# Gated linear attention ahead of a multiplicative FFN: part 1 in units of two batches and four heads, two positions on a partition, all small products by quarters of the array

## The chip, the cores and the metric

The kernel runs on one core of one Trainium2 chip. The metric is the device time of one execution in microseconds (us). Before the change it is 507.3 us, the median of three runs (506.86 to 508.71). A run counts as slow when it is over 1.5% above the fastest of the same kernel; only fast runs are compared.

Ratios below are the mean time of one kernel's fast runs over the mean of the fast runs of the kernel before from the same rounds, on the same chip, with a 95% interval. They are therefore not quite the ratios of the medians that are quoted beside them.

Names used throughout: TensorE is PE in the profile (PEld its weight loads), VectorE DVE, ScalarE ACT, GpSimd POOL, and SP the engine that here does nothing but issue transfers. A q after the name (SPq, ACTq) is that engine's sequencer. L128 is line 128 of the kernel in question.

## The reference, cut to what matters

```python
# 4 batches, 8 heads, 768 positions, 48 numbers per head
for t in range(S):
    state = alpha[:, :, t, :, None] * state + np.einsum('bhd,bhe->bhde', k[:, :, t], v[:, :, t])
    y[:, :, t] = np.einsum('bhd,bhde->bhe', q[:, :, t], state)
x = y.transpose(0, 2, 1, 3).reshape(3072, 384)
out = ((x @ w1) * (x @ w2)) @ w3 @ w_out          # weights given as float64
```

## The kernel before

Part 1 does the recurrence in chunks of 128 positions. A unit is one batch and one chunk with all eight heads: 24 units. For each unit the logarithms of alpha are summed over the positions with a triangular matrix on TensorE (decays), k and q are scaled by the exponentials, transposed, multiplied (scores), masked, and multiplied with v (attend). The state that comes from earlier chunks adds its part (state) and is brought forward (outer, advance). The results are stored in DRAM (xd) and read back transposed (xT) for the gates, the products x@w1 and x@w2 in three fp32r parts. Gate tiles are slipped between the units to fill TensorE, and the float64 weights (raw) are converted on ScalarE and VectorE meanwhile. What follows part 1 (rest of the gates, the product of w3 and w_out, the projection) keeps its arithmetic; each tile of the output is stored in two transfers where it was one.

```python
def load_kq(n):                                   # one load: 128 positions x 8 heads x 48
    st["kq", n] = inp.tile([C, 2, H, D], FP32, tag="kq", name="kq")
    nc.sync.dma_start(out=st["kq", n][:, 0], in_=rows(k, n))
    nc.sync.dma_start(out=st["kq", n][:, 1], in_=rows(q, n))
...
def decays(n):                                    # one running sum over 128 positions
    lc = bank()[:, 0:DM]
    ...
    if n < LATE:
        nc.tensor.matmul(lc, utri if n % 2 else after, la, start=True, stop=True)
    else:
        for i in range(2):
            nc.tensor.matmul(lc, sums[:, n % 2], la[:, i], start=(i == 0), stop=(i == 1))
...
def attend(n):
    ...
    for i in range(2):
        nc.scalar.copy(x[:, :, i], y[i])
    ...
    for half in range(2):                         # two stores a unit, issued by ScalarE
        nc.scalar.dma_start(out=to[half, :, :, ds(c * C, C)], in_=x[ds(DP * half, D)])
```

A point that matters later: the order in which each engine gets its instructions is laid down when the kernel is built, from an estimate of when each will be ready. It is not simply the order of the program text. TensorE's order here is nearly that of the text (at most one place off); of SP's loads those of the raw weights are put up to 47 places ahead of it, those of q, k, v and alpha at most 8 (all counted on the built program).

Of the kernel before, what the change touches and what calls it, by code (L numbers as in the profile page):

```python
# [46 lines left out]

@with_exitstack
def kernel(
# [19 lines left out]
    NP = H // 2  # L69
# [10 lines left out]
    assert DM <= 512 and TG <= 512  # L80
# [11 lines left out]
    ps = pool("ps", 8, space=PSUM)  # L92
# [6 lines left out]
    work = pool("work", 2, stack=part1, side="right", reuse_waits="tile")  # L99

    def bank():
        return ps.tile([C, 512], FP32, tag="bank", name="bank")
# [6 lines left out]
    ends = {n: dram.tile([3, DM], FP32, name=f"ends{n}") for n in range(2, N, 2) if n % NCH}  # L109
    xd = [dram.tile([DM, TG], FP32, name=f"xd{g}") for g in range(NG)]  # L110
    abd = [dram.tile([C, KF, TG], FP32, name=f"abd{g}") for g in range(NG)]

    vs = [p1.tile([C, H, DP], FP32, name=f"v{i}") for i in range(AHEAD + 1)]
    for x in vs:
        nc.gpsimd.memset(x[:, :, D:], 0.0)

    def rows(src, n):
        b, c = divmod(n, NCH)
        return src[b, :, ds(c * C, C), :].rearrange("h p d -> p h d")

    def load_a(n):
        if n < N:
            st["a", n] = inp.tile([C, H, D], FP32, tag="ac", name="ac")
            nc.sync.dma_start(out=st["a", n], in_=rows(alpha, n))

    def load_kq(n):
        if n >= N:
            return  # L128
        st["kq", n] = inp.tile([C, 2, H, D], FP32, tag="kq", name="kq")
        nc.sync.dma_start(out=st["kq", n][:, 0], in_=rows(k, n))  # L130
        nc.sync.dma_start(out=st["kq", n][:, 1], in_=rows(q, n))

    def load_v(n):
        if n < N:
            st["v", n] = vs[n % len(vs)]
            nc.sync.dma_start(out=st["v", n][:, :, 0:D], in_=rows(v, n))
# [15 lines left out]
    utri = p1.tile([C, C], FP32, name="utri")  # L152
    after = p1.tile([C, C], FP32, name="after")

    sums = p1.tile([C, 2, C], FP32R, name="sums")
    keep = p1.tile([C, C], I32, name="keep")
    qks = [p1.tile([C, 2, H, DP], FP32, name=f"qk{i}") for i in range(3)]
    Ts = [p1.tile([C, NP, DP], FP32, name=f"T{i}") for i in range(2)]
    decs = [p1.tile([C, 3, NP], FP32, name=f"dec{i}") for i in range(2)]

    make_upper_triangular(nc, utri, val=1.0, diag=True)

    nc.vector.tensor_scalar_add(after, utri, -1.0)
    nc.gpsimd.tensor_copy(out=sums[:, 0], in_=after)
    nc.gpsimd.tensor_copy(out=sums[:, 1], in_=utri)
    nc.vector.memset(rebias, -(1023.0 - 127.0) * 2.0 ** 23)

    nc.vector.tensor_scalar_mul(keep, utri, -1.0)
    keep_bc = keep[:, None, :].to_broadcast([C, NP, C])
    for x in qks:  # L170
        nc.vector.memset(x[:, :, :, D:], 0.0)
    make_identity(nc, ident)
    for x in Ts + decs:
        nc.gpsimd.memset(x, 0.0)
# [55 lines left out]
    def last(n):  # L230
        return n % NCH == NCH - 1

    def logs(n):
        if n >= N:
            return
        a = st.pop(("a", n)).rearrange("p h d -> p (h d)")
        la = st["la", n] = work.tile([C, DM], FP32, tag="la", name="la")
        nc.scalar.activation(la, a, AF.Ln)
        if n >= LATE:

            t = st["la", n] = work.tile([C, 2, DM], FP32R, tag="la2", name="la2", bufs=1)
            nc.scalar.copy(t[:, 0], la)
            nc.vector.tensor_sub(t[:, 1], la, t[:, 0].bitcast(FP32))
        if n in ends:
            nc.scalar.dma_start(out=ends[n][2:3], in_=a[0:1])

    def decays(n):
        if n >= N:
            return
        lc = bank()[:, 0:DM]  # L250
        la = st.pop(("la", n))
        if n < LATE:
            nc.tensor.matmul(lc, utri if n % 2 else after, la, start=True, stop=True)
        else:
            for i in range(2):
                nc.tensor.matmul(lc, sums[:, n % 2], la[:, i], start=(i == 0), stop=(i == 1))  # L256

        e = st["e", n] = work.tile([C, 2, DM], FP32, tag="e", name="e", bufs=3)
        nc.scalar.activation(e[:, 0], lc, AF.Exp, scale=-1.0)
        nc.scalar.activation(e[:, 1], lc, AF.Exp)  # L260
        if n in ends:
            nc.scalar.dma_start(out=ends[n][0:1], in_=e[0:1, 0])
        if n + 1 in ends:
            nc.scalar.dma_start(out=ends[n + 1][1:2], in_=e[C - 1:C, 1])

    def decayed(n):
        if n < N:
            nc.vector.tensor_mul(qks[n % 3][:, :, :, 0:D], st.pop(("kq", n)),
                                 st.pop(("e", n)).rearrange("p i (h d) -> p i h d", h=H))

    def load_ends(n):
        if n not in ends:
            return
        with nc.allow_non_contiguous_dma(reason="single values to partitions"):
            for i in range(2):
                nc.scalar.dma_start(out=decs[n // 2 % 2][ds(DP * i, D)].rearrange("d m j -> d (m j)"),
                                    in_=ends[n].rearrange("m (j i d) -> i d (m j)", i=2, d=D)[i])

    def transposed(n):
# [3 lines left out]
        qkT = work.tile([C, 2, NP, C], FP32, tag="qkT", name="qkT")  # L283

        tp = [bank().rearrange("p (i j c) -> p i j c", i=2, j=NP) for _ in range(2)]
        for i in range(2):
            for j in range(NP):
                for half in range(2):
                    s = ds(DP * half, DP)
                    nc.tensor.transpose(tp[half][:, i, j, :], qk[s, i, 2 * j:2 * j + 2, :], ident[s, s])  # L290
        for half in range(2):
            nc.scalar.copy(qkT[:, :, :, ds(DP * half, DP)], tp[half])  # L292
        st["qkT", n] = qkT

    def outer(n):
        if n >= N or last(n):
            return
        qk, vc = qks[n % 3], st["v", n]
        s1 = bank()[:, 0:NP * D].rearrange("p (j d) -> p j d", j=NP)
        for j in range(NP):  # L300
            for i in range(2):
                nc.tensor.matmul(s1[ds(DP * i, DP), j, :], qk[:, 0, 2 * j + i, :], vc[:, 2 * j + i, 0:D],  # L302
                                 start=True, stop=True)

        if n % 2:
            to = st["T", n] = work.tile([C, NP, D], FP32, tag="tmp", name="tmp")
        else:
            to = Ts[1][:, :, 0:D]
        if n % NCH == 0:
            nc.vector.tensor_copy(out=to, in_=s1)  # L310
        else:
            nc.vector.tensor_add(to, s1, Ts[n % 2][:, :, 0:D])

    def advance(n):

        if n not in ends:
            return
        dec, d = work.tile([C, NP], FP32, tag="dec", name="dec"), decs[n // 2 % 2]
        nc.gpsimd.tensor_mul(dec, d[:, 0, :], d[:, 1, :])
        nc.gpsimd.tensor_mul(dec, dec, d[:, 2, :])  # L320
        nc.gpsimd.tensor_tensor(Ts[0][:, :, 0:D], st.pop(("T", n - 1)),
                                dec[:, :, None].to_broadcast([C, NP, D]), op=ALU.mult)

    def scores(n):
        qkT = st["qkT", n]
        sc = [bank().rearrange("p (j c) -> p j c", j=NP) for _ in range(2)]
        for j in range(NP):
            for i in range(2):
                r = ds(DP * i, D)
                nc.tensor.matmul(sc[i][:, j, :], qkT[r, 0, j, :], qkT[r, 1, j, :], start=True, stop=True)  # L330
        ms = work.tile([C, 2, NP, C], FP32, tag="ms", name="ms")
        for i in range(2):
            nc.vector.tensor_tensor(ms[:, i].bitcast(I32), sc[i].bitcast(I32), keep_bc, op=ALU.bitwise_and)  # L333
        st["ms", n] = ms

    HP = NP // 2

    def attend_state(n):
        qkT = st.pop(("qkT", n))
# [3 lines left out]
        y = [bank()[:, 0:HP * C].rearrange("p (j c) -> p j c", c=C) for _ in range(2)]  # L343
        st["y", n] = y, [(half * HP + j, i, y[i][ds(DP * half, DP), j, :])
                         for j in range(HP) for i in range(2) for half in range(2)]
        if n % NCH:
            for j, i, to in st["y", n][1]:
                r = ds(DP * i, D)
                nc.tensor.matmul(to, Ts[n % 2][r, j, :], qkT[r, 1, j, :],  # L349
                                 start=(j % HP == 0), stop=False, skip_group_check=True)  # L350

    def attend(n):
        (y, heads), ms, vc = st.pop(("y", n)), st.pop(("ms", n)), st.pop(("v", n))
        for j, i, to in heads:
            nc.tensor.matmul(to, vc[:, 2 * j + i, :], ms[:, i, j, :], start=(n % NCH == 0 and j % HP == 0),  # L355
                             stop=(j % HP == HP - 1), skip_group_check=True)
        x = work.tile([C, HP, 2, C], FP32, tag="x", name="x")
        for i in range(2):
            nc.scalar.copy(x[:, :, i], y[i])
        x = x.rearrange("p j i t -> p (j i) t")  # L360

        g, c = divmod(n, G)
# [254 lines left out]
```

## Time and profile before

| | before |
|---|---|
| median time | 507.3 us |
| TensorE busy / mean granted clock | 466.6 us / 0.973 |
| VectorE, ScalarE busy | 371.3, 248.1 us |
| TensorE idle in part 1 | 35.6 us, 34.8 of it before 145 us |
| issues of loads of q, k, v, alpha on SP | 96, 84.8 us in all |
| issues by ScalarE in part 1 | 91, 33.2 us in all |
| packets of the inputs | 98,304 of 192 B |

The line below is the stretch from 145 to 212 us, the last 67 us of part 1 (length, then busy us of PE, weight loads, DVE, ACT, POOL, then granted clock, DMA share, GB/s).

```profile
145.00:212.00 67.00, 66.17 (x861) 60.45 (x861) 44.45 (x74) 37.50 (x85) 3.43 (x9) 1.00 0.57 138
```

TensorE is busy 66.17 of 67.00 us at full clock: whatever the transfers do in this stretch costs nothing.

### The profile page before, as it was taken

Reading aid. Unit: us, or ns where it says so; the run is one execution under the profiler, and the core shown is the slowest. Engines: PE = TensorE matmul, PEld = TensorE weight load, DVE = VectorE, ACT = ScalarE, POOL = GpSimd, SP = SyncE. Lnnn points to the kernel's source line nnn. Section 1 sums busy time; section 2 is a strip of 40 time slices with the busy share of each in tenths; the row PEclk is TensorE's granted clock in tenths of the full one; section 3 lists DMA queues with packets and bytes.
Section 4 is the critical chain, followed back from the end, with each engine's and each line's share of the span. In section 5 each row is a group of like instructions: output and inputs, shape, how many; then the busy total and the mean of one; then the engine's idle time right before and its main releaser. Section 6 shows DMA issues by size and latency. Waiting matters only on the chain.

```text
span 506.9 us, 9883 instructions
## 1 busy us (share of the span) xinstructions
PE 466.6 (92%) x3760; PEld 424.8 (84%) x3760; DVE 371.3 (73%) x620; ACT 248.1 (49%) x479; POOL 13.8 (3%) x43
## 2 busy tenths in 40 slices
PE   3777499499799999999999999999999999999997
PEld 1556388398799899899999998898888799999996
DVE  2777789699966767599999976967533497777771
ACT  2665566468557555355555544544323343333330
POOL 2000000010100010000000000000000000000000
PEclk9998599889899999999999999999999999999999
DMA  9999999998879833265565432432001686555511
GB/s 173 182 217 196 256 216 225 194 246 209 166 167 215 194 81 106 79 186 174 177 200 186 160 117 88 142 103 72 33 31 48 171 231 192 174 180 179 174 56 47
DMA packets 168735, 79.10 MB, mean 156 GB/s; under 512 B 112856, under 2 KB 162544, under 8 KB 168688
## 3 DMA queue, kind: packets, MB, share of 16 engines
q1 hardware_dynamic: 147184, 70.73, 54.9%
q10 hardware_dynamic: 21504, 7.75, 6.7%
q8 instruction: 29, 0.48, 0.4%
q14 instruction: 18, 0.15, 0.1%
HBM read 56.40 MB, written 22.06 MB: 155 GB/s over the span
## 4 chain that ended last, share of the span: by engine, by line
PE 71%; DVE 1%; issue 0%; ACT 0%; DVEq 0%
PE bank L387 36%; PE bank L391 18%; PE bank L436 8%; PE bank L355 2%; PE bank L330 2%; PE bank L430 1%; PE bank L349 1%; PE bank L290 1%; PE bank L302 1%; PE bank L256 1%; DVE x L378 1%; DVE x L377 0%; ACT t L389 0%; ACT ab L454 0%; DVE r L392 0%
## 5 line engine op out<-in xcount | busy, mean ns | idle before, releaser
L387 PE MATMUL bank<-x,w 128*128 128x384 f32 x768 | 163.9, 348 | 15.0 <-DVE x L377 8.5
L387 PEld LDWEIGHTS bank<-x,w 128*128 128x128 f32 x768 | 136.5, 192 | 21.1 <-DVE x L377 9.7
L389 ACT ACTIVATE t<-bank 128x384 f32<-128x384 f32 x152 | 73.4, 490 | 119.2 <-PE bank L387 96.7
L392 DVE SCALAR_TENSOR_TENSOR r<-bank,t 128x384 f32<-128x384 f32 x128 | 68.4, 550 | 45.7 <-ACT t L389 37.1
L391 PE MATMUL bank<-x,w 128*128 128x384 f32 x384 | 89.2, 340 | 1.5 <-DVE x L378 1.4
L391 PEld LDWEIGHTS bank<-x,w 128*128 128x128 f32 x384 | 69.2, 191 | 3.1 <-PE bank L387 1.4
L387 PE MATMUL bank<-w3o,ab 128*128 128x384 f32 x384 | 70.6, 335 | 1.0 <-ACT ab L454 1.0
L387 PEld LDWEIGHTS bank<-w3o,ab 128*128 128x128 f32 x384 | 66.8, 188 | 1.4 <-ACT ab L454 1.3
L436 PE MATMUL bank<-wo,w3T 128*128 128x384 f32 x128 | 42.6, 486 | 0.0
L391 PE MATMUL bank<-w3o,ab 128*128 128x384 f32 x192 | 37.1, 334 | 0.0
L436 PEld LDWEIGHTS bank<-wo,w3T 128*128 128x128 f32 x128 | 24.2, 189 | 14.9
L189 ACT ACTIVATE rest<-raw 128x512 f32<-128x512 uint32 (+1 forms) x36 | 23.4, 649 | 26.6 <-DMA raw<-in_moe_w_dram 18.3
L455 DVE TENSOR_TENSOR ab<-abl,ab 128x1024 fp32r<-128x1024 f32 x24 | 29.4, 1223 | 9.1 <-ACT ab L454 9.1
L403 DVE TENSOR_TENSOR ab<-r 128x384 f32<-128x384 f32 x64 | 35.3, 552 | 0.9
L454 ACT ACTIVATE ab<-abl 128x1024 fp32r<-128x1024 f32 x24 | 25.5, 1062 | 20.1 <-PE bank L391 18.8
L330 PEld LDWEIGHTS bank<-qkT 48*128 48x128 f32 x384 | 25.5, 198 | 10.8 <-ACT qkT L292 5.1
L330 PE MATMUL bank<-qkT 48*128 48x128 f32 x384 | 30.7, 298 | 4.2 <-ACT qkT L292 3.7
L333 DVE TENSOR_TENSOR ms<-bank,keep 128x512 int32<-128x512 int32 x48 | 31.2, 682 | 4.2 <-PE bank L330 4.2
L391 PEld LDWEIGHTS bank<-w3o,ab 128*128 128x128 f32 x192 | 33.6, 188 | 0.0
L292 ACT COPY qkT<-bank 128x512 f32<-128x512 f32 x48 | 25.8, 586 | 10.3 <-PE bank L290 8.8
L194 ACT ACTIVATE power<-power,rebias 128x512 uint32<-128x512 uint32 (+1 forms) x36 | 25.0, 696 | 10.3 <-DVE power L193 10.3
L392 DVE SCALAR_TENSOR_TENSOR o<-bank,t 128x384 f32<-128x384 f32 x24 | 13.4, 556 | 22.1 <-issue 13.7
(65 smaller groups left out, 509.7 us busy)
## 6 DMA issues: line engine op xcount, KB each, us to landing
abd<-ab SPq DMA_DIRECT2D x64, 192.0 KB
abl<-abd SPq DMA_DIRECT2D x24, 512.0 KB
raw<-in_moe_w_dram SPq DMA_DIRECT2D x16, 512.0 KB
raw<-in_moe_w_dram SPq DMA_DIRECT2D x24, 256.0 KB
ac<-in_alpha_dram SPq DMA_DIRECT2D x24, 192.0 KB
kq<-in_k_dram SPq DMA_DIRECT2D x24, 192.0 KB
kq<-in_q_dram SPq DMA_DIRECT2D x24, 192.0 KB
v<-in_v_dram SPq DMA_DIRECT2D x24, 192.0 KB
```

The costliest lines, as they stand in the source:

```text
L194: nc.scalar.activation(power, power, AF.Relu, scale=2.0 ** 23, bias=rebias)
L292: nc.scalar.copy(qkT[:, :, :, ds(DP * half, DP)], tp[half])
L330: nc.tensor.matmul(sc[i][:, j, :], qkT[r, 0, j, :], qkT[r, 1, j, :], start=True, stop=True)
L333: nc.vector.tensor_tensor(ms[:, i].bitcast(I32), sc[i].bitcast(I32), keep_bc, op=ALU.bitwise_and)
L387: nc.tensor.matmul(p1, w[part][i], x[part][i], start=(part == i == 0), stop=(part == 1 and i == n - 1))
L389: nc.scalar.activation(t, p1, AF.Copy, scale=(1.0 + 1.0 / P) * scale)
L391: nc.tensor.matmul(p2, w[2][i], x[2][i], start=(i == 0), stop=(i == n - 1))
L392: nc.vector.scalar_tensor_tensor(to, p2, -scale, t, op0=ALU.mult, op1=ALU.add)
L403: nc.vector.tensor_mul(ab, *r)
L436: nc.tensor.matmul(po, w3T[:, j, :], wo[:, j, :], start=(j == 0), stop=(j == KF - 1))
L454: nc.scalar.activation(t[:, 0], ab, AF.Copy, scale=1.0 - 2.0 ** -13)
L455: nc.vector.tensor_sub(t[:, 1], ab, t[:, 0].bitcast(FP32))
```

## The change

Intent: put two neighbouring positions of a batch side by side on a partition, so that a run in DRAM is 384 B and not 192 B; put two batches on the two halves of the partitions, with four heads a unit; then do all small products on quarters of the array, so that TensorE changes its mode less often. y gets two banks of its own, and the schedule of the gates is retuned. The core of the diff:

```diff
-    ps = pool("ps", 8, space=PSUM)
+    ps = [pool("ps", 6, space=PSUM)]
+    yp = pool("yp", 2, stack=part1, space=PSUM)
...
+    def load(dst, src, n):
+        b0, c, hh = n // NU * W, n % NU // 2, n % 2
+        src = src[ds(b0, W), ds(hh * HH, HH), ds(c * C, C), :]
+        for b in range(W):
+            nc.sync.dma_start(out=dst[ds(b * DP, DP)], in_=src[b].rearrange("h (p r) d -> p h (r d)", r=R))
...
-            nc.scalar.dma_start(out=ends[n][2:3], in_=a[0:1])
+            for b in range(W):
+                nc.scalar.dma_start(out=ends[n][2:3, b].rearrange("o (h d) -> o h d", d=D),
+                                    in_=a[b * DP:b * DP + 1, :, 0:D])
...
-            nc.tensor.matmul(lc, utri if n % 2 else after, la, start=True, stop=True)
+        for x in parts:
+            nc.tensor.matmul(lc.rearrange("p (r x) -> p r x", r=R), w[:, 0],
+                             x[:, None, 0:DH].to_broadcast([C, R, DH]), ...)
+        for x in parts:
+            nc.tensor.matmul(lc[:, DH:], w[:, 0], x[:, DH:], ...)
+        for x in parts:
+            nc.tensor.matmul(lc[:, 0:DH], w[:, 1], x[:, DH:], ...)
...
-                nc.tensor.matmul(sc[i][:, j, :], qkT[r, 0, j, :], qkT[r, 1, j, :], start=True, stop=True)
+                        nc.tensor.matmul(sc[i][rows(b), s, j, :], qkT[f, b, 0, j, rows(s)], qkT[f, b, 1, j, :],
+                                         start=True, stop=True)
...
+        for b in range(W):
+            for i in range(2):
+                nc.scalar.dma_start(out=dst[hh, i, b], in_=x[ds(DP * (b ^ i), D), i])
-        for half in range(2):
-            nc.scalar.dma_start(out=to[half, :, :, ds(c * C, C)], in_=x[ds(DP * half, D)])
```

Attend, outer (now called add) and state are cut into quarters in the same way as the scores. The order inside a unit is now: half of the scores, attend of the unit before, the other half, add, state, transposes, gates, decays.

## The prediction

> **What bounds the kernel now.** I read the page's row of slices first, then the busy time by stretches, then who waited for whom, then the timeline of TensorE in one unit of part 1. The slices (12.7 us each):
>
> ```profile
> PE   3777499499799999999999999999999999999997
> DVE  2777789699966767599999976967533497777771
> PEclk9998599889899999999999999999999999999999
> DMA  9999999998879833265565432432001686555511
> ```
>
> Two regimes. In the first ten or eleven slices (to about 130 us) the DMA engines are full, TensorE has holes and its granted clock dips. From there to the end TensorE is at 9 in every slice but the last. Part 1, which the change rewrites, ends at about 212 us, so it lies in both. The other 295 us (the rest of the gates, the fold of w3 and w_out, the projection) are TensorE work that the change leaves alone. The stretches of the first regime:
>
> ```profile
> 20.00:44.00 24.00, 19.62 (x327) 15.34 (x322) 18.86 (x33) 14.45 (x32) 2.06 (x6) 1.00 1.04 196
> 44.00:66.00 22.00, 13.72 (x102) 10.46 (x100) 17.34 (x28) 13.94 (x28) 0.00 (x0) 0.61 1.07 236
> 66.00:88.00 22.00, 21.35 (x277) 19.49 (x268) 19.91 (x38) 15.02 (x34) 0.95 (x3) 1.00 1.10 230
> 88.00:106.00 18.00, 11.00 (x114) 9.16 (x116) 11.98 (x20) 8.12 (x18) 2.53 (x3) 0.81 1.03 199
> 106.00:128.00 22.00, 21.19 (x283) 19.52 (x276) 22.00 (x43) 16.74 (x38) 0.00 (x0) 1.00 0.90 222
> ```
>
> Columns: length, then busy us of PE, weight loads, VectorE, ScalarE, GpSimd, then granted clock, DMA share, GB/s. The holes are in 44 to 66 (8.3 us idle, clock 0.61) and 88 to 106 (7.0 us, 0.81), with DMA over 1.0 in both. What they wait for:
>
> ```profile
> ACT rest L189 <- DMA raw<-in_moe_w_dram: 18.3, 10, 2.8
> ACT la L238 <- DMA ac<-in_alpha_dram: 14.0, 6, 3.1
> DVE mant L190 <- DMA raw<-in_moe_w_dram: 13.0, 4, 4.8
> 57.20 1.33 PE L387 MATMUL bank<-x,w 128*128 128x384 f32 x3 [4.78 <-ACT x L376]
> 100.28 1.33 PE L387 MATMUL bank<-x,w 128*128 128x384 f32 x3 [4.84 <-DVE x L377]
> ```
>
> TensorE waits for the split of x, but the split stands in line on VectorE and ScalarE, whose instructions ahead of it wait for weights or alpha still in transfer. So there DMA is the cause at one remove. TensorE's idle before 145 us, gap by gap, adds up to 34 us; some 10 us more go to a low clock (the 16 score matmuls at 47.59 took 2.08 us, at 66.16 they took 1.16).
>
> The second regime, one unit of part 1:
>
> ```profile
> 190.80 0.51 PE L256 MATMUL bank<-la,sums 128*128 128x384 f32 x2
> 191.23 0.67 PE L349 MATMUL bank<-qkT,T 48*64 48x128 f32 x16
> 191.83 1.16 PE L330 MATMUL bank<-qkT 48*128 48x128 f32 x16
> 192.83 0.66 PE L290 MATMUL bank<-ident,qk 64*128 64x64 f32 x16
> 193.42 1.09 PE L355 MATMUL bank<-ms,v 128*64 128x128 f32 x16
> 194.34 0.62 PE L302 MATMUL bank<-v,qk 128*64 128x48 f32 x16
> 194.90 1.31 PE L387 MATMUL bank<-x,w 128*128 128x384 f32 x6
> ```
>
> Start to start: decays 0.43, state 0.60, scores 1.00, transposes 0.59, attend 0.93, outer 0.55: 4.10 us of small products per unit; the two half gates after them make a unit of 7.3 us, and TensorE has no hole in it.
>
> **What the Trainium skill says.** (1) "DMA: Bandwidth & Descriptors", Specifications: line rate needs transfers of at least 512 B. The trace agrees: the 98,304 packets of 192 B (q, k, v, alpha) took 17.7 ns each, 10.8 bytes per ns; the 33,792 of 512 B took 30.0 ns, 17 bytes per ns. (2) The same page, on why a DMA increments its semaphore by 16: the number of engines is set by the slowest dimension, so a transfer to 64 partitions should still use 16; no run here shows it yet. (3) "TensorEngine Tiling (Array Packing)", Key Properties: changing the tiling mode drains TensorE. The trace agrees: from the last state group (quarters) to the first score (halves) 0.20 us pass, within state a group follows in 0.109. (4) "TensorE: Matmul & The Clock Gate", Part 3: tiles in different places run at once. The trace agrees: in state four quarter matmuls start within 20 ns, the next four 109 ns later; in scores and attend two half-array matmuls per 112 and 109 ns; in outer (48 columns) two per 58 ns.
>
> **The change, part by part.**
>
> *Inputs.* Two positions side by side make runs of 384 B, so 49,152 packets in place of 98,304. On the line through 192 B (17.7 ns) and 512 B (30.0) a 384 B packet is estimated at 25 ns. The inputs then take 49,152 x 25 = 1,230 us of engine time, not 1,743: 32 us less over 16 engines, of which some 20 us before 106 us (about 62,900 of the packets are there). DMA share there falls from about 1.05 to 0.85. Issues on SP double (96 to 192) but each writes a quarter of the descriptors (unloaded issues took 0.37 us, in a full queue 0.7 to 0.8), so SP's time stays.
>
> *Small products by quarters.* An fp32 product is two instructions. Scores go from 16 to 32, attend from 16 to 32, outer from 16 to 32, state stays 16. But each is a quarter of the array, four at a time: scores 8 groups x 0.109 = 0.87 (pure time before 8 x 0.112 = 0.89), attend 0.87 (0.87), state 4 x 0.109 = 0.44, outer 8 groups x 0.058 = 0.46 if four weight loads overlap as well as two do. Total 2.64 against 2.66: **the array gains nothing**. What is gained is a mode: full, quarters, rows, columns, full before (four switches), full, quarters, rows, full after (three). At 0.1 to 0.2 us a switch with its refill that is about 0.2 us a unit.
>
> *Decays.* The running sum over pairs takes three products (384, 192, 192 columns) for one of 384: twice the columns. In fp32 (the first ten units) 2 x 0.32 us become 1.28, +0.64 warm, nearly twice that at a cold clock: +6.4 us, in the first regime, and for units 0 and 1 on the starting chain (L253 took 1.65 us there). In fp32r (14 units) 2 x 0.173 become 0.35 plus four of about 0.09: +0.35 a unit, +4.9 us where TensorE is full.
>
> *State from zeros.* Attend_state now runs for the first units of a batch pair too: 4 x 0.44 = 1.8 us.
>
> Sum in the full regime: a unit goes from 4.10 to about 4.2 us: -0.2 (switch) +0.35 (decays) -0.02; over 14 units about +2, with two of the zero states +3.
>
> *PSUM.* y has two banks of its own; six are left for what used eight with y among them. Attend_state(n) needs both y banks evicted after attend(n-1): half the scores and add lie between, 0.44 + 0.46 = 0.90 us, while the end of the last matmul (0.27) and two copies (0.67) with signals take about 1.05. A wait of 0.1 to 0.3 us a unit, longer where ScalarE is behind: 2 to 4 us.
>
> *ScalarE* issues four stores of x for two and more boundary rows: some 75 issues more at 0.25 to 0.4 us. It was occupied about 70% in part 1 with issues counted, so mostly hidden. VectorE's elements are the same, two small adds for one.
>
> *First regime.* With less DMA the wait for weights at 91 to 95.5 us (4.75) and 52 to 55 us (3.1) should mostly go, and the low clock after them: about 8 to 9 us. The start gains 1 to 2 us in arrivals and loses as much to longer cold decays. The stretch 20 to 44 gains 1 to 2, 66 to 88 and 106 to 128 nothing: TensorE and VectorE (22.00 of 22.00) are full there. Together -11 us after the fp32 decays.
>
> **Sum.** 507 - 11 + 3 + 3 = 502. The schedule was retuned with the change (where gates begin, one extra half gate at two places, four at the end of part 1), which should recover a little of the waits: I say 500.5.
>
> **The rivals.**
> - *DMA was the whole bound of the first regime.* For: share at or above 1.0 to 106 us. Then 20 us come off, and the total is about 490. Against: in that time VectorE had about 76 of 106 us busy and TensorE 75, and both get more to do, so they bind after some 12 us.
> - *VectorE binds first.* For: 22.00 of 22.00 in 106 to 128, and the conversions are paced by units, not by transfers. Then the holes only move, and TensorE's extra work shows: 505 to 508.
> - *TensorE's extra work is larger than I count.* fp32r with 192 columns may not run at the rate of 384 (nothing in the trace has that shape); at a fourth of the rate it adds 14 x 0.9 = 13 us in the full regime: about 514. Or the outer groups fall to two at a time: +0.46 x 20 = 9 us. The order of quarters, pinned in the program, speaks against the second.
> - *PSUM waits.* Six banks in rotation tie the gates to VectorE's masks and ScalarE's copies; 0.5 us a unit would be +12 us. Against: VectorE is 70% busy after 130 us.
>
> **Range and chances.** The mechanism gives 502 with about 7 us either way, mostly from how much of the 44 us of holes and low clock goes. Faster by over 2% means under 497.2; that takes 15 us or more from the first regime, or waits that are nil: 0.33. Slower by over 2% (over 517.4) takes slow fp32r and PSUM waits together: 0.07. Within 2%: 0.60. Eight in ten: 489 to 511.
>
> **What would show it.** Right: 49,152 packets of 384 B near 25 ns; DMA share under 0.9 before 106 us; waits on raw weights and alpha below half of 45 us; a unit after 130 us of 7.3 to 7.6 us with four quarter matmuls per 0.109 us; the three decays at 0.75 to 0.8 us. Wrong: packets of 384 B that take 30 ns or more; fp32r products of 192 columns over 0.2 us apart; holes on TensorE before attend_state or the gates in every unit; the holes at x's split as long as before.

## More of the kernel before

The next line is from the waits of SP's queue (us in total, times, longest).

```profile
SPq L130 <- DMA xd<-x: 5.4, 2, 3.1
```

SP stood 5.4 us in all for the stores of x (xd<-x) that ScalarE issues. That is odd at first sight, since a load needs nothing of a store; keep it in mind. The page's list of transfers gives the size of a load:

```profile
ac<-in_alpha_dram SPq DMA_DIRECT2D x24, 192.0 KB
```

## The result, and the profile after

The changed kernel takes 563.31 us (median of 4 runs, 560.43 to 566.7) where the kernel before takes 507.55 in the same rounds: ratio 1.1099 (1.1032 to 1.1165). It is slower by 11%, and correct.

| | before | after |
|---|---|---|
| span of the profiled run | 506.9 | 562.2 |
| TensorE busy / mean granted clock | 466.6 / 0.973 | 499.4 / 0.946 |
| start of unit 6, 10, 23 (its first scores) | 66.2, 106.3, 205.8 | 76.3, 122.6, 260.0 |
| TensorE idle in part 1 | 35.6 | 58.4 |
| loads of q, k, v, alpha on SP | 96, 84.8 us | 192, 124.9 us |
| issues by ScalarE in part 1 | 91, 33.2 us | 166, 76.8 us |
| packets of the inputs | 98,304 at 17.7 ns | 49,152 at 24.6 ns |

From the start of unit 23 on both kernels need the same time (301 and 302 us), so all of the loss lies in part 1: 16 us of it stand at the start of unit 10, and 38 more come from unit 10 to 23, where 7.7 us a unit became 10.6. The span grew by 55.3 us, of which 32.8 are TensorE busy and 22.5 idle. Of the busy part, up to 17 us is a lower clock: (1 - 0.946) x 562.2 = 30.4 us lost against (1 - 0.973) x 506.9 = 13.7 (an estimate, since some of it falls on idle time).

The slices of the kernel after (14.1 us each), to set beside those of the prediction:

```profile
PE   4767669889788788779999999999999999999996
...
PEclk9797878979898989968999999999999999999999
DMA  5556656555575656631365555433210287566531
```

The DMA engines are no longer full anywhere in part 1: 5 to 7 where there was 9. But TensorE now has holes in the first eighteen slices. Part 1 from 145 us on, in numbers:

```profile
145.00:212.00 67.00, 57.02 (x952) 51.55 (x953) 43.35 (x78) 32.16 (x70) 2.78 (x6) 0.92 0.62 158
212.00:262.00 50.00, 40.30 (x647) 36.07 (x645) 24.26 (x47) 21.49 (x48) 2.02 (x6) 0.86 0.48 132
```

TensorE is busy 57 of 67 us where it was busy 66, at a clock of 0.92 and 0.86 where it was 1.00, and the DMA share is 0.48 to 0.62. None of them is full. One unit, on TensorE (start, length, engine, line, operation; in brackets the idle time ahead of it and what ended it):

```profile
190.03 0.51 PE L278 MATMUL bank<-la,sums 128*128 128x384 f32 x2
...
190.89 0.67 PE L357 MATMUL bank<-qkT 48*64 48x128 f32 x16
191.38 1.05 PE L413 MATMUL y<-ms,v 64*48 64x128 f32 x32
192.25 0.62 PE L357 MATMUL bank<-qkT 48*64 48x128 f32 x16
192.69 0.63 PE L373 MATMUL bank<-v,qk 64*64 64x48 f32 x32
197.62 0.94 PE L402 MATMUL y<-qkT,T 48*64 48x128 f32 x16 [4.30 <-ACT x L418]
```

The products themselves are as predicted: two halves of the scores at 0.49 and 0.44 us, attend 0.87, add 0.45 when nothing stands in its way, the three decays 0.86 start to start. Then comes a hole of 4.3 us ahead of state (L402). The waits of the other engines, over the whole run:

```profile
PE y L402 <- ACT x L418: 22.1, 12, 4.3
...
PE bank L278 <- ACT la L255: 20.8, 7, 5.0
...
ACT rest L209 <- DMA raw<-in_moe_w_dram: 17.5, 13, 2.6
...
ACT la L255 <- DMA ac<-in_alpha_dram: 9.9, 5, 3.3
...
DVE mant L210 <- DMA raw<-in_moe_w_dram: 7.1, 6, 2.6
```

The second line of these is new; the first is what the prediction called the wait for the y banks. But the last three say what stands behind them: ScalarE and VectorE, in line, still wait for loads. Follow the hole at 193 to 197 us back. First ScalarE:

```profile
194.82 0.67 ACT L209 ACTIVATE rest<-raw 128x512 f32<-128x512 uint32 x1 [2.50 <-DMA raw<-in_moe_w_dram]
...
196.50 0.72 ACT L214 ACTIVATE power<-power,rebias 128x512 uint32<-128x512 uint32 x1 [1.00 <-DVE power L213]
197.13 0.62 ACT L418 COPY x<-y 128x256 f32<-128x256 f32 x2
197.51 1.83 ACTq L424 DMA_DIRECT2D xd<-x  x4
```

It copies y (L418) at 197.13, because the two instructions ahead of it, of the conversion of weights, came late: L209 waited 2.50 us for raw weights, L214 another 1.00 for VectorE. The last line is four issues by which ScalarE is held up again, 1.83 us. SP issued these raw weights here:

```profile
187.54 2.09 SPq L128 DMA_DIRECT2D kq<-in_q_dram  x2
189.68 1.08 SPq L201 DMA_DIRECT2D raw<-in_moe_w_dram  x2
```

In the trace the first of the two q loads starts at 187.54, and the store of x that ScalarE had issued at 185.24 landed at 187.52; the second starts at 189.03, and the store issued at 185.66 landed at 189.02. Both times the load and the store raise the same semaphore. So the raw weights were issued at 189.68 and 190.32, the second landed at 194.74, and TensorE stood. The two waits add 0.42 and 0.63 us here, and 4.4 us go from the second issue of the weights to its landing: a single hole doesn't show which of the links counts. What SP waits for, over the whole run:

```profile
SPq L128 <- DMA xd<-x: 20.8, 15, 4.5
...
SPq L128 <- DMA xT<-xd: 8.8, 2, 4.4
SPq L128 <- DMA dec<-ends: 8.1, 4, 3.3
...
SPq L128 <- DMA ends<-e: 6.4, 7, 2.4
```

The issue records name a semaphore for each transfer. SP and ScalarE together use eight, in turn, in the order that the build laid down, and most issues wait for the transfer that used the same one before them (after, 364 of SP's 390 issues and 130 of ScalarE's 170 carry that wait, counted on the built program). In the kernel before, 45 of the 235 issues of part 1 come within 0.5 us of the landing that frees their semaphore; after, 110 of 403 do. The size of a load, and the count:

```profile
ac<-in_alpha_dram SPq DMA_DIRECT2D x48, 96.0 KB
```

Half the bytes each, but the issue is not shorter. A load alone, after a pause on SP, took 0.37 us before and 0.60 after; the mean of all issues is 0.88 and 0.65 us. Four times 0.88 are 3.5 us a unit, eight times 0.65 are 5.2. That alone does not fill SP: it issues for 56% of part 1 both before (118 of 212 us) and after (147 of 262 us). The rest of its time it waits.

### The profile page after: what moved, and what is told of

It reads as the page before. It is cut to its first block, busy times and chain, and to the rows that moved or that the text cites. A ratio compares the mean times of both kernels' runs of the same rounds, so it can differ in the third digit from the quotient of the medians.

```text
span 562.2 us, 12721 instructions
## 1 busy us (share of the span) xinstructions
PE 499.4 (89%) x5008; PEld 454.4 (81%) x5008; DVE 376.5 (67%) x642; ACT 252.6 (45%) x479; POOL 15.4 (3%) x53
## 4 chain that ended last, share of the span: by engine, by line
PE 55%; DVE 0%; issue 0%; DVEq 0%
PE bank L451 30%; PE bank L455 15%; PE bank L500 7%; PE bank L494 1%; PE y L413 1%; PE bank L357 1%; PE y L402 0%; PE bank L341 0%; DVE o L456 0%; DVEq L456 0%
## 5 line engine op out<-in xcount | busy, mean ns | idle before, releaser
L451 PE MATMUL bank<-x,w 128*128 128x384 f32 x768 | 166.7, 352 | 6.9 <-ACT x L440 3.7
L451 PEld LDWEIGHTS bank<-x,w 128*128 128x128 f32 x768 | 138.2, 194 | 13.3 <-ACT x L440 4.7
L456 DVE SCALAR_TENSOR_TENSOR r<-bank,t 128x384 f32<-128x384 f32 x128 | 69.6, 554 | 62.3 <-ACT t L453 37.1
L455 PE MATMUL bank<-x,w 128*128 128x384 f32 x384 | 90.3, 343 | 1.9 <-DVE x L442 1.7
L455 PEld LDWEIGHTS bank<-x,w 128*128 128x128 f32 x384 | 70.5, 194 | 3.5 <-PE bank L451 3.1
L278 PE MATMUL bank<-la,sums 128*128 128x384 f32 x48 | 21.0, 520 | 21.8 <-ACT la L255 20.8
L209 ACT ACTIVATE rest<-raw 128x512 f32<-128x512 uint32 (+1 forms) x36 | 23.4, 650 | 33.6 <-DMA raw<-in_moe_w_dram 17.5
L357 PE MATMUL bank<-qkT 48*64 48x128 f32 x768 | 35.9, 300 | 1.8 <-ACT qkT L344 0.9
L402 PE MATMUL y<-qkT,T 48*64 48x128 f32 x320 | 18.2, 307 | 18.8 <-ACT x L418 18.6
L214 ACT ACTIVATE power<-power,rebias 128x512 uint32<-128x512 uint32 (+1 forms) x36 | 25.0, 697 | 17.4 <-DVE power L213 16.8
```

What stands on the lines that cost most here:

```text
L214: nc.scalar.activation(power, power, AF.Relu, scale=2.0 ** 23, bias=rebias)
L357: nc.tensor.matmul(sc[i][rows(b), s, j, :], qkT[f, b, 0, j, rows(s)], qkT[f, b, 1, j, :], start=True, stop=True)
L451: nc.tensor.matmul(p1, w[part][i], x[part][i], start=(part == i == 0), stop=(part == 1 and i == n - 1))
L455: nc.tensor.matmul(p2, w[2][i], x[2][i], start=(i == 0), stop=(i == n - 1))
L456: nc.vector.scalar_tensor_tensor(to, p2, -scale, t, op0=ALU.mult, op1=ALU.add)
```

## The experiments

Eighteen kernels were run, each with a profile and three rounds. The expectations use letters for the theories: S, the transfers (their number, SP's and ScalarE's issues and the eight shared semaphores); P, TensorE and its hand-overs with ScalarE and VectorE; in the first round also the y banks and the running sums; O and H are told where they come up. The runs are called by their first letter below, the pinned ones (p_) by their order. Results first:

| run | what | us (median) | ratio to before (95%) |
|---|---|---|---|
| (the change) | | 563.31 | 1.1099 (1.1032, 1.1165) |
| a_state_later | state moved behind a half gate | 562.54 | 1.1045 (1.0984, 1.1105) |
| b_one_decay | one running sum of three, wrong | 550.88 | 1.0855 (1.0811, 1.0899) |
| c_stores_pool | stores of x issued by GpSimd | 562.30 | 1.1026 (1.0948, 1.1105) |
| d_raw_pool | raw weights issued by GpSimd | 562.32 | 1.1064 (1.1022, 1.1105) |
| k_one_load | one load for two, wrong | 545.45 | 1.0732 (1.0699, 1.0765) |
| g_act_issues_pool | all ScalarE's issues to GpSimd | 543.61 | 1.0711 (1.0656, 1.0766) |
| m_one_load_pool | k and g together, wrong | 530.59 | 1.0444 (1.0402, 1.0486) |
| u_all_three | k, g and b together, wrong | 532.21 | 1.0477 (1.0428, 1.0526) |
| q_busy | g with idle copies on ScalarE | 566.71 | 1.1146 (1.1101, 1.1192) |
| e_before_split | before, loads in two by partitions | 554.14 | 1.0901 (1.0862, 1.0941) |
| n_split_heads | before, loads in two by heads | 518.27 | 1.0177 (1.0138, 1.0216) |
| o_split_pool | e, second halves by GpSimd | 524.84 | 1.0314 (1.0284, 1.0345) |
| s_before_act_pool | before, ScalarE's issues to GpSimd | 506.13 | 0.9949 (0.9918, 0.9980) |
| p_after_in_k_order | the change in k's order | 579.32 | 1.1356 (1.1288, 1.1423) |
| p_k_in_after_order | k in the change's order | 550.72 | 1.0817 (1.0751, 1.0882) |
| p_e_in_n_order | e in n's order | 544.81 | 1.0718 (1.0661, 1.0774) |
| p_n_in_e_order | n in e's order | 554.57 | 1.0908 (1.0848, 1.0969) |
| p_g_in_after_order | g in the change's order | 543.54 | 1.0674 (1.0610, 1.0738) |

### First round: taking single stalls away

Moving state behind the first half gate gives ScalarE time to copy y.

```diff
         add(n)
-        attend_state(n)
-        transposed(n + 1)
         run(n - 1 not in begin)
+        attend_state(n)
+        transposed(n + 1)
```

> The changed kernel, with attend_state (and the transposes behind it) moved behind the first half gate of the unit, so that the two y banks have 1.6 us longer to be copied out. Theory Y (the two y banks and the in-order ScalarE are the main cost: 21.7 us of TensorE gaps stand before attend_state): those gaps shrink to under 6 us and the time falls by 12 to 20 us, to about 545 to 550, two more mode switches a unit (about 4 us) counted. Theory Q (queues and waits for transfers set the pace, the y wait is only where the delay shows): the gaps turn up in front of the next thing and the time stays within 5 us of 563.

562.54 us: nothing. Its profiled run was a slow one; in it the wait ahead of state was 13 us and not 22. The fast runs alone (558 to 563 us) show that the wait for the y banks is not the main cost; a gain of a few us, set off by the two more mode switches, they can't tell.

Only the first of the three running sums (the result is wrong, relative error 1.12):

```diff
-                             start=(x is parts[0]), stop=False, skip_group_check=True)
-        for x in parts:
-            nc.tensor.matmul(lc[:, DH:], w[:, 0], x[:, DH:], ...)
-        for x in parts:
-            nc.tensor.matmul(lc[:, 0:DH], w[:, 1], x[:, DH:], ...)
+                             start=(x is parts[0]), stop=(x is parts[-1]), skip_group_check=True)
```

> Wrong result on purpose: the running sums of the decays use the first of their three products alone, so as many columns as before the change. Theory D (TensorE's own extra work is the cost): 0.43 us x 14 units + about 0.67 x 10 units = 13 us and more with the low clock, so about 548. Theory Y or Q (TensorE waits for others anyway): most of it is taken up by longer waits, 3 to 7 us, so 556 to 560.

550.88 us, 12 less. The prediction had 6.4 + 4.9 = 11.3 for these products. A reserve holds for all runs of the first three rounds: each was built anew, and none was pinned (see the fourth round). Built again, 193 of VectorE's 642 instructions and 184 of ScalarE's 478 (issues left out) stand at another place in b than in the changed kernel, in c 130 and 57, in d 263 and 250.

The stores of x, then the raw weights, issued by GpSimd in place of ScalarE and SP:

```diff
-                nc.scalar.dma_start(out=dst[hh, i, b], in_=x[ds(DP * (b ^ i), D), i])
+                nc.gpsimd.dma_start(out=dst[hh, i, b], in_=x[ds(DP * (b ^ i), D), i])
```

> The four stores of x per unit are issued by GpSimd instead of ScalarE, which spends 49.5 us issuing them (19.7 before the change). Theory Q (ScalarE in order, clogged by issues): the gaps before attend_state and before the decays both shrink, 10 to 20 us, to about 545 to 553. Theory Y alone: the copies of y come before their own stores and gain little, under 5 us.

```diff
-            nc.sync.dma_start(out=raw[:, ds(i * m, m)], in_=src)
+            nc.gpsimd.dma_start(out=raw[:, ds(i * m, m)], in_=src)
```

> The loads of the raw weights are issued by GpSimd instead of standing in SP's queue behind eight half loads of inputs per unit at 0.6 us each. Theory W (ScalarE and VectorE stand still at the conversions because their weights were issued late): the waits of ScalarE for raw weights (17.5 us) and much of the gaps behind them go, 10 to 20 us, about 545 to 553. If the order of the queue doesn't matter: within 4 us of 563.

562.3 us both: nothing. In c ScalarE has 47 of its 76.8 us of issues taken off, and yet the time stays. SP's waits in c show that the place of the stores was taken by the small boundary rows (ends), which ScalarE still issues:

```profile
SPq L128 <- DMA ends<-e: 26.0, 9, 8.5
```

Theory W falls with d. The raw weights no longer stand in SP's queue, and ScalarE waits for them as long as before (17.5 us):

```profile
ACT rest L209 <- DMA raw<-in_moe_w_dram: 17.8, 9, 3.3
```

### Second round: the number of transfers

The cleanest test of theory S leaves the change out: in the kernel before, each load is cut into two of 64 partitions. Packets, bytes and all products stay.

```diff
+    def two(to, x):
+        for i in range(2):
+            nc.sync.dma_start(out=to[ds(i * DP, DP)], in_=x[ds(i * DP, DP)])
-            nc.sync.dma_start(out=st["a", n], in_=rows(alpha, n))
+            two(st["a", n], rows(alpha, n))
     (k, q and v likewise)
```

> The kernel before with every load of q, k, v and alpha cut into two transfers of 64 partitions (96 loads become 192, as the change has; packets, bytes and all products as before). Theory S (the number of transfers: SP and ScalarE share eight completion semaphores, so twice the loads means that each issue waits for a transfer that began more recently, and what stands behind the issue waits too): 515 to 535 us, part 1 ending at 220 to 240 instead of 212. Rival P (the change loses on TensorE and on its hand-overs with ScalarE and VectorE, the transfers don't matter): 505 to 510 us.

554.14 us: 46 us, more than the theory asked for, and nearly the whole loss of the change without any of it. P falls as the only cause. (Whether the transfers do it or the order that the build gave them is the question of the fourth round.)

The counterpart in the changed kernel: one load of 128 partitions, the same bytes and packets of 384 B, the second batch replaced by more rows of the first (wrong):

```diff
-        src = src[ds(b0, W), ds(hh * HH, HH), ds(c * C, C), :]
-        for b in range(W):
-            nc.sync.dma_start(out=dst[ds(b * DP, DP)], in_=src[b].rearrange("h (p r) d -> p h (r d)", r=R))
+        src = src[b0, ds(hh * HH, HH), ds(min(c, NCH - 2) * C, 2 * C), :]
+        nc.sync.dma_start(out=dst, in_=src.rearrange("h (p r) d -> p h (r d)", r=R))
```

> The changed kernel with each load in one transfer of 128 partitions in place of two of 64: the same bytes and the same 384 B packets, 96 loads in place of 192, all the rest as it is. The second batch's rows are replaced by more rows of the first, so the result is wrong on purpose. Theory S: 530 to 550 us, SP's waits for ScalarE's stores and boundary rows under half. Rival P: 560 to 566 us.

545.45 us, 18 less. SP's waits for the stores of x fall as expected; at the line of the loads 20.8 us became:

```profile
SPq L127 <- DMA xd<-x: 2.9, 4, 1.0
```

Then every transfer that ScalarE issues in part 1 to GpSimd, whose transfers show eight semaphores of their own in the trace (stores, boundary rows, decay columns, loads of x; all six lines changed like the one of c):

> The changed kernel with every transfer that ScalarE issues in part 1 (stores of x, boundary rows, decay columns, loads of x for the gates) issued by GpSimd, which has eight completion semaphores of its own. Nothing of the result changes. Theory S (SP and ScalarE hold each other up through shared semaphores): 525 to 550 us, and SP waits for no store. Rival 1 (SP's own chain of twice as many loads is enough): 555 to 566. Rival P: 558 to 566, with the waits for ScalarE's arithmetic as long as before.

543.61 us, 20 less, and correct. And both together:

> Both of the two before it: each load one transfer (wrong result on purpose), and ScalarE's transfers issued by GpSimd. Theory S: 515 to 535 us, what is left over 507 being the twelve of the decays and a few of the y banks. Rival P: 558 to 566.

530.59 us: 33 of the 56 us come back, nearly the sum of the two (18 + 20 = 38).

### Third round: what about a transfer costs

Loads cut by heads and not by partitions, in the kernel before:

```diff
-            nc.sync.dma_start(out=to[ds(i * DP, DP)], in_=x[ds(i * DP, DP)])
+            nc.sync.dma_start(out=to[:, ds(i * (H // 2), H // 2)], in_=x[:, ds(i * (H // 2), H // 2)])
```

> The kernel before with each load in two again, now by heads: 128 partitions of four heads each in place of 64 partitions of eight heads. Bytes, packets and the number of transfers are those of e_before_split (554 us). If the count of transfers is the cause (theory S): 540 to 560 us. If it is what a transfer to 64 partitions costs at the issue (at least 0.595 us there, 0.367 for 128 partitions) or in the engines it uses: 510 to 525 us.

518.27 us, 9 and not 46 more than before. So twice the count is the smaller part; the form to 64 partitions, or what the build makes of it, is the larger. Both forms have 512 runs of 192 B a transfer. On SP alone after a pause the issue takes 0.37 us by heads, as a whole load does, and 0.60 us by partitions; back to back on SP 0.51 and 0.63 (medians).

The second halves issued by GpSimd:

```diff
-            nc.sync.dma_start(out=to[ds(i * DP, DP)], in_=x[ds(i * DP, DP)])
+            (nc.sync, nc.gpsimd)[i].dma_start(out=to[ds(i * DP, DP)], in_=x[ds(i * DP, DP)])
```

> e_before_split with the second half of each load issued by GpSimd, which has completion semaphores of its own: SP issues 96 loads as in the kernel before, each half still has 64 partitions. If SP's issues or the shared eight semaphores are the cause: 505 to 515 us. If it is the transfers to 64 partitions themselves (fewer engines at work, slower landing): 535 to 560 us.

524.84 us, between the two theories. TensorE was busy only 0.4 us in the first 20 us (9.0 in the kernel before), since GpSimd issues loads before it makes the triangular constants; that may explain about 8.5 of the 15.5 us (an estimate: 9.0 - 0.4). With the issues spread over two engines the transfers of 64 partitions keep the DMA engines full again (share 1.08, 1.00 and 1.14 in the first three stretches of 20 us, where e has 0.70, 0.65 and 0.88). So the engines can carry transfers of this form at a full share; in e they are issued too late for it.

ScalarE's issues of the kernel before to GpSimd:

> The kernel before with every transfer that ScalarE issues in part 1 issued by GpSimd. In the changed kernel this was worth 20 us. Theory S: in the kernel before 45 of 235 issues come within half a microsecond of the landing that frees their semaphore, so it should gain some too: 497 to 506 us, the only candidate so far that beats both kernels. If TensorE and the full DMA engines leave nothing to gain: 505 to 510 us.

506.13 us against 509.31 in the same rounds, ratio 0.9949 (0.9918 to 0.9980). It beats both kernels, by half a per cent: in the kernel before there is little to free.

And g with a copy on ScalarE for each issue taken off it:

```diff
+    def busy():
+        nc.scalar.copy(idle[:, 1], idle[:, 0])
...
+                busy()
                 nc.gpsimd.dma_start(out=dst[hh, i, b], in_=x[ds(DP * (b ^ i), D), i])
```

> g_act_issues_pool (543.6 us) with a copy of 128x384 on ScalarE, about 0.49 us that nobody waits for, at each place where an issue was taken off it: ScalarE's time is as in the changed kernel, the shared semaphores are still relieved. If the gain of g was the time that the issues took on ScalarE: back to 557 to 566 us. If it was the shared semaphores: 541 to 549 us.

566.71 us, which looks like a verdict for ScalarE's time. It isn't one. The copies wait for nothing, so the build put them early: 138 of the 165 ran before 120 us, and ScalarE was occupied 0.88 to 0.97 of the time in the three stretches of 20 us to 60 us. The changed kernel's issues are spread evenly (82 before 140 us, 84 after). The run is inconclusive.

### Fourth round: the transfers or the order of the build

That copy was a warning. Counting on the built programs showed that e and n do not differ in their transfers only: with loads to 64 partitions SP's loads of raw weights are put at most 15 places ahead of the program text and those of the inputs nowhere, by heads up to 77 and 15, and ScalarE's and VectorE's orders differ too. In the changed kernel it is 17 and none, in k 61 and 7. So two theories: O, the loss through the loads is the order that the build lays down; H, the hardware pays for the transfers. To part them, each engine's instructions were pinned to a given order by edges without any wait:

```python
for engine, order in ORDER.items():        # order: places in the program text, taken from another build
    for a, b in zip(order, order[1:]):
        tc.add_manual_dep(insts[engine][b], insts[engine][a].name, deps, reason="pin")
```

The orders of the pinned builds were compared with those asked for and are the same on every engine that was pinned.

> The changed kernel with all its own transfers and products (correct), each engine's instructions pinned to the order that k_one_load (545 us) had, in which the loads run further ahead. Theory O (the loss through the loads is the order that the build laid down, not the transfers): 543 to 550 us. Theory H (the hardware pays for two loads to 64 partitions: 0.6 us an issue on SP, shared semaphores): 557 to 568 us.

> e_before_split (loads cut by partitions, 554 us) pinned to the order of n_split_heads (loads cut by heads, 518 us). Theory O: 516 to 524 us. Theory H: 545 to 558 us.

> The cross-check: n_split_heads (loads cut by heads, 518 us) pinned to the order of e_before_split (554 us). Theory O: 545 to 556 us. Theory H: 514 to 524 us.

> k_one_load (one load in place of two, 545 us, wrong result on purpose) pinned to the order of the changed kernel (563 us), whose loads run less far ahead. If the transfers are what costs: 543 to 552 us. If the order of the build is what costs: 558 to 568 us. After the pair of the kernel before, where either alone was enough to cost (545 and 555 for 518): 555 to 565 us.

| order of the build | the change's loads (two) | one load |
|---|---|---|
| the change's | 563.3 | 550.7 |
| k's | 579.3 | 545.5 |

| order of the build | before, by partitions | before, by heads |
|---|---|---|
| e's | 554.1 | 554.6 |
| n's | 544.8 | 518.3 |

O falls for the changed kernel: in k's order it becomes slower by 16 us, and in its own order one load instead of two is worth 12.6 of the 18 us. In the kernel before it is neither alone. In n's order the loads by partitions cost 26.5 us, in e's order nothing, because that order has already lost 36 us with any loads. Where the form costs time, SP's waits in the first 250 us of e in n's order look like those of the changed kernel:

```profile
SPq L132 <- DMA xd<-x: 15.9, 8, 3.3
```

At last, g in the order of the changed kernel:

> g_act_issues_pool (ScalarE's transfers issued by GpSimd, 543.6 us) with TensorE, VectorE, ScalarE's arithmetic and SP pinned to the order of the changed kernel (563 us). If g's 20 us were the relief of ScalarE: 541 to 549 us. If they were another order: 557 to 566 us.

543.54 us, the same as g. The 20 us are from the issues that ScalarE no longer makes, not from another order. The longest of SP's waits for transfers in it:

```profile
SPq L136 <- DMA ends<-ac: 7.6, 2, 5.6
```

No store of x is left there.

One sum sets the runs side by side: how long SP's loads of inputs and weights stood for transfers that ScalarE (or GpSimd in its place) issues and that they do not need (stores of x, decay rows, decay columns, x for the gates; the lines of SP's waits added up).

| run | us (median) | SP's loads stood for them, us |
|---|---|---|
| before | 507.6 | 5 |
| n (before, by heads) | 518.3 | 6 |
| e (before, by partitions) | 554.1 | 61 |
| the change | 563.3 | 48 |
| c, d | 562.3, 562.3 | 51, 62 |
| k | 545.5 | 17 |
| g, m | 543.6, 530.6 | 0, 0 |
| e in n's order | 544.8 | 25 |
| n in e's order | 554.6 | 4 |
| the change in k's order | 579.3 | 28 |

c and d leave these waits as long or longer and gain nothing; k takes most of them away, g and m all. So far the sum goes with the times. But n in e's order and the change in k's order are slow with less of it: the order of the build costs time in another way, which no run here shows.

### The account

> The changed kernel with the three named causes taken away together: one load in place of two, ScalarE's transfers issued by GpSimd, only the first running-sum product (wrong result on purpose, in two ways). If they add up and nothing else of weight is left: 514 to 522 us (530.6 of m_one_load_pool less the 12 of b_one_decay), what stays over 507 being the wait for the y banks, the states from zeros and a lower clock. If the running sums lie beside other work once the rest is gone: 527 to 532 us. If the waits feed each other, so that the last one pays more than its share: 503 to 512 us.

532.21 us, where m_one_load_pool had 530.59. Once the transfers are relieved, the two running sums are worth nothing that shows. So the 12 us of b are not to be added to the 33. But the remedy brought a stall of its own, in one place. In u:

```profile
67.47 1.31 PE L397 MATMUL y<-qkT,T 48*64 48x128 f32 x16 [16.39 <-ACT x L413]
```

16.39 us ahead of one state product, for the copy of y on ScalarE. And on ScalarE:

```profile
65.91 1.16 ACT L435 ACTIVATE x<-xT 128x1152 fp32r<-128x1152 f32 x1 [15.09 <-DMA xT<-xd]
66.97 0.63 ACT L413 COPY x<-y 128x256 f32<-128x256 f32 x2
```

The copy stands behind the first split of x, which began 15.09 us after the instruction before it, when the load of x (xT) had landed. GpSimd issued that load at 60.41, in line behind boundary rows and stores. In m the same stall is 11.0 us. Without it m would be at about 519 and u at about 516 (estimates: 530.6 - 11.0 and 532.2 - 16.4, if nothing else moves). Some 10 us over the kernel before then stay unexplained. Neither run was pinned.

## Why the prediction was wrong

It said 500.5 us with 489 to 511 for eight in ten; it was 563.3, and the chance given to slower by over 2% was 0.07.

- **A slip in its sum.** The gains that it lists for the first regime are 8 to 9 and 1 to 2 us, at most 11 before the 6.4 us of the fp32 running sums. It says -11 after them. The start, which it sets at nil, holds one to three of the 6.4 already (units 0 and 1); with the rest taken off, some -4 to -7 are left, and the sum is about 507 and not 502. Beside the 56 us that is small.
- **Packets and DMA share: right.** 49,152 packets of 384 B at 24.6 ns (said: 25); share 0.46 to 0.69 in stretches of 20 us of part 1 (said: under 0.9, about 0.85). That the share fell so far is no gain: 22,500 packets had begun by 106 us, where half of the prediction's 62,900 were to be expected. The loads came late.
- **Products by quarters: right.** Four every 0.109 us; the array gains nothing. Products of 192 columns in fp32r are 0.089 us apart. The three decays take 0.86 us start to start, somewhat over the 0.75 to 0.8.
- **Decays: right in size, as far as it shows.** 11.3 us were said, 12 came back when they were taken out alone; none when the transfers were relieved.
- **The step that failed: "Issues on SP double (96 to 192) but each writes a quarter of the descriptors [...] so SP's time stays."** The issues took 124.9 us and not 84.8: a transfer to 64 partitions took 0.60 us at the least where one to 128 partitions, with four times the descriptors, took 0.37. One load in place of two brings back 18 us, 12.6 of them in the same order of the build. SP was not full before or after (56% of part 1); what the prediction left out is that most issues also wait for an earlier transfer on one of eight shared semaphores: SP's loads stood 48 us and not 5 for transfers of ScalarE that they don't need.
- **The second step that failed, of the same kind: ScalarE's "some 75 issues more at 0.25 to 0.4 us [...] mostly hidden".** The count was right (91 to 166), the time was not: 33.2 to 76.8 us, 43.6 more. The boundary rows of alpha alone went from 0.24 to 0.59 us each (medians). Taken off ScalarE they are worth 20 us, in the same order too.
- **First regime, -11 us: wrong.** It took the load on the DMA engines for the cause of the late weights. Their share fell and the waits stayed long: those on raw weights and alpha, which should have fallen below half of 45 us, are 34.5 (17.5 + 9.9 + 7.1), and unit 6 starts 10 us later.
- **Full regime, +3 us: wrong.** It took TensorE to stay full there, at 4.1 to 4.2 us of small products a unit. The products came out so, but from unit 10 to 23 a unit takes 10.6 us and not 7.7: 38 of the 56 us, with holes such as the 4.3 us ahead of state.
- **The y banks, 2 to 4 us: as a wait too small (22.1 us), as a cause not shown.** Moving state away from it changed nothing that the runs can tell, and with ScalarE's issues gone (g) the wait is 4.7 us.
- **The rivals.** All four were about TensorE, VectorE, the banks or the DMA engines' share. None was about issuing, though the profile of before showed loads standing for stores.

Shown are: that taking away the two loads to 64 partitions and ScalarE's issues together brings back 33 of the 56 us (m, not pinned), that ScalarE's part is not the order of the build, and that the first is mostly not (12.6 of 18 us). Left open: how the 20 us part into ScalarE's own time and the eight shared semaphores (c speaks for the semaphores, since 47 us of the time were taken off, SP's waits stayed, and nothing came of it; q, which was to settle it, failed); how an order of the build costs time; why the form with 64 partitions takes longer to issue; the running sums, worth 12 us alone and nothing once the transfers were relieved; and the last 10 us.

## What to carry to other kernels

Count the transfers and not only their bytes: a layout that needs two transfers where one did doubles the issues, and an engine that computes and also issues has them in line with its arithmetic. When a wait names a store that the waiting load does not need, look at the semaphore that the two share; taking one of two coupled queues away may show nothing until the other goes too. Before reading an experiment, compare the order of the built program with that of the kernel it is set against, and pin it if it differs.

## What the Trainium skill lacked or had wrong

- "DMA: Bandwidth & Descriptors", section Issuing engines are not separate DMA queues, says that issuing from several engines saves only the sequencer's time, "which is usually small relative to the DMA itself". Here the issuing engine mattered: 166 issues took 76.8 us of ScalarE, and moving them to GpSimd gained 20 us, through that time or through the semaphores that ScalarE and SP share (not parted here).
- No page gives the time of an issue by the form of the transfer. "Perfetto Trace Analysis", section DMA Instruction — HWDGE, says that the profile's length of an issue holds the wait for the shared generator, its use and the push of the semaphore. The runs show at least 0.37 us for 128 partitions (512 or 1024 runs) and 0.60 for 64 (256 or 512 runs): it does not follow the number of runs.
- "DMA: Bandwidth & Descriptors", section Why a DMA increments its semaphore by 16 and not by 1, asks for a semaphore per transfer in flight. It doesn't say what few of them cost when two queues take turns: in the changed kernel 110 of 403 issues of part 1 come within 0.5 us of the landing of an earlier transfer on the same semaphore, and SP waited 20.8 us at one line for stores that its loads don't need.
- The same section's rule of 16 engines for 64 partitions fits the runs but isn't proved by them: with half loads from two queues the DMA share was 1.00 to 1.14, and the first 256 packets of the changed kernel, all of one load to 64 partitions, had up to 20 in flight at once, where the first 256 of a load to 128 partitions had up to 18 before the change. The trace doesn't name the engine of a packet.
- The Specifications of that page (line rate from 512 B) fit the packets: 10.8 bytes per ns at 192 B, 15.6 at 384 B (24.6 ns). They did not decide the time: the share fell from over 1.0 to under 0.7 and the kernel became slower.
